# Windowed attention in a fused three-stage kernel: the division moved from the weights to the output, and each engine's order written as a list

## The chip, the cores and the metric

The kernel runs on one core of one Trainium2 chip. The metric is the device time of one execution in microseconds (us), the median of several runs. Engines are named as in the profile: PE (TensorE; PEld is its weight load), DVE (VectorE), ACT (ScalarE), POOL (GpSimd), SP (the queue that issues most DMAs).

## The reference, cut to what matters

```python
# q, k, v: (4, 8, 576, 64), float32
scores = q @ k.T / sqrt(64) - slope[h] * |i - j|      # kept where 0 <= i - j < 128
attn = exp(scores - max)
attn = attn / (sum(attn) + 1e-9)
x = (attn @ v).transpose(0, 2, 1, 3).reshape(4, 576, 512)
x = x + relu(layer_norm(x) @ w_ch1) @ w_ch2           # 512 -> 2048 -> 512
h = relu(x @ w_in)                                    # 512 -> 1024
out = (h * sigmoid(conv3(h))) @ w_out                 # 1024 -> 512
```

The four weight matrices and the convolution's weights come in as 64-bit floats and are turned into float32 on the chip, in integer steps on halves of the words.

## The kernel before, in words

**Attention** comes first. Its unit is a tile: 128 query rows of two heads. Two batches of 576 rows make a block of 9 tiles, and 2 blocks of batches times 4 pairs of heads give 72 tiles. A round of the loop at L873 takes four tiles, as two halves a and b, so there are 18 rounds. For one half:

- `turn_qk`: 8 transposes on PE of q and k into a PSUM buffer (`ps_r`, tag `ptr`), copied out by ACT (`copy_turned`).
- `scores`: 16 products and 8 bias products on PE (64x64 pieces) into `ps_s`; `join` and `minima` on DVE; four `exponentials` on ACT, each with its row sums.
- `shares`: 1/sum on DVE, then the weights `pp` times it, three of the four pieces on DVE (L787), one on POOL (L788).
- `turn_p`: 4 transposes; `copy_p` on ACT; `select_p`: two masks on POOL (L810); `values`: up to 16 products on PE (128x64 pieces) into `po`; `outputs`: copy on ACT into `x`, once a round.

The rounds overlap: round n holds the scores of round n, the turning of P of n-1 and the values of n-2. Every engine takes its instructions in the order in which the loop body calls them; the list of calls is the schedule.

**Beside it** twelve pieces of `w_ch1` and `w_ch2` are loaded (0.5 MB each, SP) and turned into two float32r parts. A piece that is loaded in half-round o has its steps in half-rounds o+3 to o+8 (`FINE_AT`, `FINE_START`): rescale on POOL (L358), three integer steps on DVE (L373, L378, L383), the high part on ACT (L412), the low part on DVE (L415). All starts o are odd, so rescale and the first DVE step stand in one round. The layer norm of the first 384 rows (`LN_ATT`) and two first blocks of the hidden layer (`hidden`) are in the attention loop too.

**After it** (from L958) a planner (`Plan.issue`) writes the rest, with PE as its fixed backbone, into the same queues behind the attention.

`extras` in a round of before calls the weight steps of its first half-round after both joins and minima, and those of the second at the end of the round, ahead of the next round's first join.

Of the kernel before, what the change touches and what calls it, by code (L numbers as in the profile page):

```python
# [210 lines left out]
def tile_kernel(  # L211
# [183 lines left out]
    FINE = (("rescale",), (0,), (1,), (2,), ("high",), ("low",))  # L395

    def weights_step(stages, start=True, only=None):

        now = [ld for ld in reversed(flight) if only in (None, ld["only"])]
        now = [(ld, ld["stages"].pop(0)) for ld in now]  # L400
        for j in range(max((len(do) for _, do in now), default=0)):
            for ld, do in now:
                if j >= len(do):
                    continue
                kind, i, raw = ld["kind"], ld["i"], ld["raw"]
                if do[j] == "rescale":
                    t = ld["t"] = fav(FA_CV0 + cvn[0] % 3 * 512, 512).bitcast(I32)
                    cvn[0] += 1
                    rescale(t, raw, G)
                elif do[j] == "high":  # L410
                    w = wtile(kind, i)
                    S.activation(w[:, 0, :], ld["t"].bitcast(F32), AF.Copy)  # L412
                elif do[j] == "low":
                    w = wtile(kind, i)
                    V.tensor_tensor(  # L415
                        out=w[:, 1, :], in0=ld["t"].bitcast(F32), in1=w[:, 0, :].bitcast(F32),
                        op=ALU.subtract,
                    )
                    flight.remove(ld)
                else:  # L420
                    to_f32(ld["t"], raw, (do[j],), ld["mid"])
        if todo and start:
            kind, i, pool = todo.pop(0)
            raw = scratch["raw"][:, scratch["n"] % 3, :]
            scratch["n"] += 1
            if kind in ("w1", "win"):
                src = (w_ch1 if kind == "w1" else w_in)[:, 2 * i * P : 2 * (i + 1) * P]
                nc.sync.dma_start(
                    raw.rearrange("p (c f) -> p c f", f=2 * P),
                    src.rearrange("(c p) f -> p c f", p=P),  # L430
                )
            else:
                src = (w_ch2 if kind == "w2" else w_out)[i * P : (i + 1) * P, :]
                nc.sync.dma_start(raw, src)
            flight.append({
                "kind": kind, "i": i, "pool": pool, "t": None, "mid": None, "only": only,
                "raw": raw.rearrange("p (n two) -> p n two", two=2), "stages": list(stages),
            })
# [98 lines left out]
    with ExitStack() as actx:  # L537
# [4 lines left out]
        ps_r = actx.enter_context(tc.tile_pool(name="ps_r", bufs=2, space=PSUM))  # L542
        ps_t = actx.enter_context(tc.tile_pool(name="ps_t", bufs=1, space=PSUM))
# [154 lines left out]
        turned = []  # L698
        live = {}

        def turn_qk(n: int):

            qt = qts[n] = apool.tile([P, W], F32, tag="qt", name=f"qt_{n}", bufs=3)
            ptr = ps_r.tile([P, 2, W], F32, tag="ptr", name=f"ptr_{n}")
            for i in range(2):
                for u in range(2):
                    bl, pr, t = seq[n + u]
                    T.transpose(ptr[:, i, u * P : (u + 1) * P], raws["qk"[i], bl, pr, t], ident)  # L708
            kd = kt[:, n % NK : n % NK + 2, :].rearrange("p u j -> p (u j)")
            turned.append((qt, ptr[:, 0], -SCALE))  # L710
            turned.append((kd, ptr[:, 1], 1.0))
# [54 lines left out]
        def exponentials(n: int, parts=range(4)):  # L766
            sc, mn = live["sc", n], live["mn", n]
            if parts[0] == 0:
                live["pp", n] = apool.tile([P, 2, 2, P], F32, tag="pp", name=f"pp_{n}", bufs=4)
                live["sm", n] = apool.tile([P, 2, 4], F32, tag="sm", name=f"sm_{n}", bufs=4)  # L770
            pp, sm = live["pp", n], live["sm", n]
            for i in parts:
# [3 lines left out]
                    accum_out=sm[:, 0, i : i + 1],  # L776
                )

        def shares(n: int):
# [4 lines left out]
            pp = live["pp", n].rearrange("p u h j -> p (u h) j")  # L784
            part = pp[:, 0:3, :]
            r = sm[:, 1, 0:3].rearrange("p (i o) -> p i o", o=1).broadcast_to([P, 3, P])
# [6 lines left out]
        def turn_p(n: int, pool=ps_t, tag="pt"):  # L793
            pp = live.pop(("pp", n))
            ptp = live["ptp", n] = pool.tile([P, 4, P], F32, tag=tag, name=f"ptp_{n}")
# [19 lines left out]
        def values(n: int):  # L815

            pt = live.pop(("pt", n))
            if n % 4 == 0:
                live["po"] = ps_o.tile([P, 4, P], F32, tag="po", name=f"po_{n}")
            po = live["po"][:, n % 4 : n % 4 + 2]  # L820
# [10 lines left out]
        def outputs(n: int):  # L831

            po = live.pop("po")
            cut = next((u for u in range(1, 4) if seq[n + u][1] != seq[n][1]), 4)
            for u0, u1 in ((0, cut), (cut, 4)):
                if u0 < u1:
                    bl, pr, t = seq[n + u0]
                    t += bl * TPB
                    S.activation(xt(t, t + u1 - u0, pr), po[:, u0:u1], AF.Copy)

        fine_at = {}
        for key, o in enumerate(FINE_START):
            for i, at in enumerate(FINE_AT):
                fine_at.setdefault(o + at, []).append((i == 0, key))
# [4 lines left out]
        def copy_turned():  # L849

            for dst, src, scale in turned[:2]:
                S.activation(dst, src, AF.Copy, scale=scale)
            del turned[:2]

        def extras(n: int, m: int):
            for args in fine_at.get(n // 2 + m, ()):
                weights_step(FINE, *args)
            for u in (n + 2 * m, n + 2 * m + 1):
                if u in SMALL_AT:
                    small_inputs(SMALL_AT.index(u))  # L860
                for stage, j in LN_ATT.get(u, ()):
                    layer_norm(0, j, stage, ps_r, "ptr")

        turn_qk(0)
        copy_turned()
        turn_qk(2)  # L870
        load_qk(*seq[TPB][:2], 0)
        load_qk(*seq[TPB][:2], 1)
        for n in range(0, NS, 4):  # L873
            a, b = n, n + 2
            before, last = n > 0, n == NS - 4
            if n // 4 < len(NB):
                keep_busy(NB[n // 4], f"a{n}")
            scores(a)
            if n > 4:
                exponentials(b - 4, range(2, 4))  # L880
            copy_turned()
            scores(b)
            if n >= 8:
                copy_p(b - 8)
                select_p(b - 8)
            if n >= 12:
                outputs(n - 12)
            join(a)
            minima(a)
            if n == 0:  # L890
                turn_qk(a + 4)
                copy_turned()
            join(b)
            minima(b)
            if n > 4:
                shares(b - 4)
            extras(n, 0)
            if n >= 8:
                values(a - 8)
                values(b - 8)  # L900
            exponentials(a)
            exponentials(b, range(2 if 0 < n and not last else 4))
# [1027 lines left out]
```

## Time and profile before

| | |
|---|---|
| median of 3 runs | 733.05 us (731.72 to 734.97) |
| profiled execution, its own time | 734.73 us |
| its span, first to last instruction | 733.0 us |
| busy share PE / PEld / DVE / ACT / POOL | 96 / 90 / 71 / 55 / 31 % |
| attention and its drain, up to the planner's first product | 148.3 us |

Busy shares are averages over stages that differ; an instruction on PE counts as busy from its start to its modelled end, so a busy PE can still have gaps between its weight loads.

### The profile page before, as it was taken

What the parts mean: (1) busy time and instruction counts of PE and PEld (TensorE: products, weight loads), DVE (VectorE), ACT (ScalarE), POOL (GpSimd) and SP (SyncE); (2) the same over time, 40 slices, a digit from 0 to 9 for tenths busy, and PEclk for the clock granted to TensorE, in tenths of its full rate; (3) what the DMA queues carried; (4) which work ended last, traced back from release to release, by engine and by line L of the source; (5) the groups of instructions that cost most, each with busy time, mean ns of one, the idle gap of its engine ahead of it and who ended that gap; (6) DMA issues with size and microseconds to landing.
All of it is one profiled execution on the core that took longest, in us unless ns stands there. A gap on an engine that the chain in (4) does not pass through costs nothing.

```text
span 733.0 us, 14382 instructions
## 1 busy us (share of the span) xinstructions
PE 706.0 (96%) x5200; PEld 657.5 (90%) x5200; DVE 520.0 (71%) x1018; ACT 402.3 (55%) x1050; POOL 230.5 (31%) x372
## 2 busy tenths in 40 slices
PE   6998888899999999999999999999999999999998
PEld 5776766699999999999999999999999899998887
DVE  6789898667888636556778655558469998786730
ACT  4887877655524323334346333344477787776741
POOL 1667688768722102221310223242421000000000
PEclk9999998999999999999999999999999999999999
DMA  6877866247529726977860699996932000000011
GB/s 145 179 186 175 201 155 190 69 156 233 179 98 306 255 77 198 299 232 238 239 207 12 179 289 280 303 279 195 265 94 80 16 30 16 29 23 22 30 54 47
DMA packets 122306, 114.69 MB, mean 156 GB/s; under 512 B 63552, under 2 KB 87292, under 8 KB 122236
## 3 DMA queue, kind: packets, MB, share of 16 engines
q1 hardware_dynamic: 101020, 76.81, 35.1%
q0 software_dynamic: 20160, 36.71, 18.1%
q8 instruction: 41, 0.67, 0.4%
q10 hardware_dynamic: 1056, 0.26, 0.2%
q14 instruction: 29, 0.24, 0.1%
HBM read 80.70 MB, written 33.05 MB: 155 GB/s over the span
## 4 chain that ended last, share of the span: by engine, by line
PE 79%; DVE 8%; POOL 4%; ACT 4%; DMA 2%; issue 2%; POOLq 0%; ACTq 0%; DVEq 0%
PE bank L1049 73%; DMA wind<-r 2%; POOL pt L810 2%; DVE ps L760 2%; ACT pp L774 1%; PE po L826 1%; DVE mn L764 1%; PE ptp L798 1%; POOL pp L788 1%; DVE pp L787 1%; PE bank L1105 1%; PE ps L734 1%; PE ptr L708 1%; ACT fa L1010 1%; DVE fa L378 1%
## 5 line engine op out<-in xcount | busy, mean ns | idle before, releaser
L1049 PE MATMUL bank<-hhr,r 128*128 128x384 f32 x1152 | 213.8, 337 | 0.5 <-DVE fa L1017 0.5
L1049 PE MATMUL bank<-r,r 128*128 128x288 f32 (+1 forms) x1248 | 204.2, 314 | 1.3 <-ACT fa L1010 1.2
L1049 PEld LDWEIGHTS bank<-hhr,r 128*128 128x128 f32 x1152 | 199.1, 188 | 2.6 <-DVE fa L1017 1.5
L1049 PEld LDWEIGHTS bank<-r,r 128*128 128x128 f32 x1248 | 193.9, 188 | 4.5 <-ACT fa L1010 2.6
L1343 POOL DMA_DIRECT2D r<-w1d x96 | 51.6, 538 | 175.1 <-PE bank L1049 158.1
L1010 ACT ACTIVATE fa<-bank 128x288 f32<-128x288 f32 (+1 forms) x112 | 49.7, 443 | 72.5 <-PE bank L1049 71.1
L1049 PE MATMUL bank<-r 128*128 128x512 f32 (+2 forms) x360 | 81.8, 372 | 0.2 <-ACT r L1793 0.2
L1049 PEld LDWEIGHTS bank<-r 128*128 128x128 f32 x360 | 63.6, 188 | 9.9 <-ACT r L1793 0.6
L1010 ACT ACTIVATE r<-fa 128x256 fp32r<-128x256 f32 (+2 forms) x94 | 47.8, 521 | 38.6 <-DMA wind<-r 12.4
L1017 DVE TENSOR_TENSOR fa<-bank,fa 128x288 f32<-128x288 f32 (+1 forms) x88 | 43.5, 500 | 25.2 <-ACT fa L1010 13.6
L1010 ACT ACTIVATE hhr<-bank 128x384 fp32r<-128x384 f32 x46 | 22.5, 490 | 68.7 <-PE bank L1049 68.5
L774 ACT ACTIVATE pp<-ps,mn 128x128 f32<-128x128 f32 x144 | 51.2, 376 | 14.8 <-DVE mn L764 12.7
L1025 DVE SCALAR_TENSOR_TENSOR fa<-fa,cw 128x576 f32<-128x576 f32 x64 | 51.2, 813 | 1.5 <-ACT fa L1010 0.7
L1017 DVE TENSOR_TENSOR r<-fa,r 128x256 fp32r<-128x256 f32 (+1 forms) x74 | 37.6, 520 | 19.3 <-ACT r L1010 13.3
L826 PE MATMUL po<-pt,rawv 128*64 128x128 f32 x544 | 38.9, 283 | 11.0 <-POOL pt L810 8.0
L1025 DVE SCALAR_TENSOR_TENSOR hhr<-bank,hhr 128x384 fp32r<-128x384 f32 x46 | 25.5, 553 | 33.8 <-ACT hhr L1010 33.8
L810 POOL TENSOR_SCALAR_AFFINE_SELECT pt<-pc 128x512 f32<-128x512 f32 x72 | 47.8, 693 | 1.8 <-ACT pc L803 1.5
L826 PEld LDWEIGHTS po<-pt,rawv 128*64 128x64 f32 x544 | 29.5, 138 | 19.9 <-POOL pt L810 17.2
L1049 PE MATMUL bank<-r,hhr 128*128 128x512 f32 (+1 forms) x192 | 44.6, 381 | 0.0
L788 POOL TENSOR_SCALAR pp<-pp,sm 128x128 f32<-128x128 f32 x36 | 34.0, 946 | 32.5 <-DVE sm L783 31.2
L1010 ACT ACTIVATE fa<-fa 128x576 f32<-128x576 f32 (+1 forms) x64 | 39.1, 620 | 2.5 <-DVE fa L1017 1.4
L1049 PEld LDWEIGHTS bank<-r,hhr 128*128 128x128 f32 x192 | 34.1, 188 | 6.7
(149 smaller groups left out, 1105.3 us busy)
## 6 DMA issues: line engine op xcount, KB each, us to landing
r<-w1d POOLq DMA_DIRECT2D x96, 256.0 KB, 4.8
fa<-in_moe_w_ch SPq DMA_DIRECT2D x24, 512.0 KB, 5.6
w1d<-r SPq DMA_DIRECT2D x40, 256.0 KB, 3.1
wind<-r SPq DMA_DIRECT2D x28, 256.0 KB, 5.0
r<-wind POOLq DMA_DIRECT2D x28, 256.0 KB, 4.9
out<-h SPq DMA_DIRECT2D x17, 256.0 KB, 2.0
rawq<-in_q SPq DMA_DIRECT2D x32, 128.0 KB, 3.4
rawv<-in_v SPq DMA_DIRECT2D x32, 128.0 KB, 3.1
```

The source lines that it names most:

```text
L378: V.scalar_tensor_tensor(out=mid, in0=raw[..., 1], scalar=-0x80000000, in1=mid, op0=ALU.bitwise_and, op1=ALU.bitwise_or,)
L708: T.transpose(ptr[:, i, u * P : (u + 1) * P], raws["qk"[i], bl, pr, t], ident)
L760: V.copy_predicated(out=sc, mask=own4, data=ps[:, :, :, P:W])
L774: S.activation(pp[:, u, h, :], sc[:, h, u], AF.Exp, bias=mn[:, h, u : u + 1], scale=-1.0, accum_out=sm[:, 0, i : i + 1],)
L788: G.tensor_scalar(out=pp[:, 3, :], in0=pp[:, 3, :], scalar1=sm[:, 1, 3:4], scalar2=1.0, op0=ALU.mult, op1=ALU.mult,)
L810: G.affine_select(out=parts[:, i], in_=pc, compare_op=ALU.is_ge, fill=0.0, base=base, pattern=[[0, 4], [sign, P]], channel_multiplier=-sign,)
L826: T.matmul(po[h * D : (h + 1) * D, u, :], rvs[bl, pr][:, t - 1 + i, h, :], pt[:, i, 2 * u + h, :], start=i == i0, stop=i == 1,)
L1010: lambda: S.activation(now(out), now(src), func, **kw),
L1017: "V", tt_ns(cols(out)), lambda: V.tensor_tensor(out=out, in0=a, in1=b, op=op),
L1025: lambda: V.scalar_tensor_tensor(out=now(out), in0=now(a), scalar=sc, in1=now(b), op0=op0, op1=op1),
L1049: T.matmul(out, lhs, now(rhs), start=start and n == 0, stop=stop and n == len(items) - 1, skip_group_check=True,)
L1343: plan.add("G", 560, lambda: nc.gpsimd.dma_start(dst, src), [src], [dst], nbytes=262144)
```

## The change

The weights `pp` go unnormalised through `turn_p`, `select_p` and `values`. `ratios` (DVE, once a round, 8 sums) makes the reciprocals; `spread` (POOL) widens them to 128x512; `spread_r` (PE) turns that with four transposes into a `ptr` buffer; `outputs` copies `po` to `x` as before, and `divide` (DVE) multiplies `x` by the turned reciprocals. `turn_p` uses the `ptr` ring, which has three buffers in place of 2 + 1. The high part of a weight piece is made by POOL, not by ACT. The loop over rounds is gone: five lists give each engine's order, a digit after a name says how many rounds behind the list's round it is, and `w0`, `w1` stand for the weight steps of the two half-rounds.

```diff
-    ps_r bufs=2, ps_t bufs=1
+    ps_r bufs=3
...
+    FINE_ON = "GVVVGV"
...
-                    S.activation(w[:, 0, :], ld["t"].bitcast(F32), AF.Copy)
+            G.tensor_copy(w[:, 0, :], ld["t"].bitcast(F32))
...
-        def shares(n: int):
+        def ratios(n: int):
             sm = live["sm", n]
             V.tensor_scalar(out=sm[:, 1], in0=sm[:, 0], scalar1=1e-9, scalar2=None, op0=ALU.add)
             V.reciprocal(out=sm[:, 1], in_=sm[:, 1])
-            V.tensor_tensor(out=part, in0=part, in1=r, op=ALU.mult)
-            G.tensor_scalar(
-                out=pp[:, 3, :], in0=pp[:, 3, :], scalar1=sm[:, 1, 3:4], scalar2=1.0,
-                op0=ALU.mult, op1=ALU.mult,
-            )
+        def spread(n: int):
+            rx = live["rx", n] = apool.tile([P, 4, 2, D], F32, tag="rx", name=f"rx_{n}")
+            G.tensor_copy(
+                out=rx, in_=live.pop(("sm", n))[:, 1].rearrange("p (h u o) -> p u h o", h=2, o=1).broadcast_to([P, 4, 2, D])
+            )
+        def spread_r(n: int):
+            rx = live.pop(("rx", n))
+            bc = live["bc", n] = ps_r.tile([P, 4, P], F32, tag="ptr", name=f"bc_{n}")
+            for u in range(4):
+                T.transpose(bc[:, u, :], rx[:, u].rearrange("p h d -> p (h d)"), ident)
...
+        def divide(n: int):
+            bc = live.pop(("bc", n))
+            for u0, u1, at in parts_of_x(n):
+                V.tensor_tensor(out=at, in0=at, in1=bc[:, u0:u1], op=ALU.mult)
...
+        ORDER = {
+            "T": "bc3 sa0 qa0 qb0 vb2 h0 pb1 pa1 sb0 va2 h1",
+            "V": "ja0 ma0 rat1 w0 w1 jb0 mb0 x2",
+            "S": "ea0.1 pcb2 w0 ea1.1 o3 pca2 eb0.1 eb1.1 cqa0 cqb0 w1",
+            "G": "ta2 w0 tb1 ex1 w1",
+            "L": "l0 w0 l1 w1",
+        }
...
+        def small_work(it):      # layer norm, yielded behind "x" of round it
...
-            scores(a)
...
-            extras(n, 1)
+        while any(streams.values()):
+            eng = min((e for e in streams if streams[e] and ready(e)), key=lambda e: streams[e][0][0])
+            _, nm, _, takes, go = streams[eng].pop(0)
+            go()
```

In the lists bc is `spread_r`, s `scores`, q `turn_qk`, v `values`, h `hidden`, p `turn_p`, j `join`, m `minima`, rat `ratios`, x `divide`, e0 and e1 the two pairs of exponentials, pc `copy_p`, o `outputs`, cq `copy_turned`, t `select_p`, ex `spread`, l the loads of q, k and v.

## Rows read from the trace of the kernel before

**Rows 1.** Windows: four stretches; busy us (xinstructions) of PE, PEld, DVE, ACT, POOL, PEclk

```profile
8.55:84.67 76.12, 66.70 (x1045) 51.87 (x1037) 63.94 (x140) 62.39 (x259) 46.90 (x67) 1.00 0.78 181
84.67:132.39 47.72, 40.43 (x581) 31.71 (x581) 43.79 (x87) 37.27 (x148) 39.05 (x51) 0.93 0.62 158
132.39:148.32 15.93, 12.96 (x133) 10.84 (x133) 8.18 (x19) 8.61 (x28) 12.10 (x19) 1.00 0.25 81
148.32:733.00 584.68, 579.05 (x3378) 556.69 (x3377) 399.42 (x754) 291.55 (x610) 130.61 (x218) 1.00 0.51 155
```

**Rows 2.** Timeline of DVE, parts of two rounds: start us, us, instruction

```profile
42.39 0.69 DVE L760 COPY_PREDICATED ps<-own,ps 128x512 f32<-128x512 int32 x1
43.12 0.69 DVE L764 TENSOR_REDUCE mn<-ps 128x4 f32<-128x512 f32 x1
43.72 0.16 DVE L782 TENSOR_SCALAR sm<-sm 128x4 f32<-128x4 f32 x1
...
44.13 0.56 DVE L787 TENSOR_TENSOR pp<-pp,sm 128x384 f32<-128x384 f32 x1
44.60 0.69 DVE L378 SCALAR_TENSOR_TENSOR fa<-fa 128x512 int32<-128x512 int32 x1
45.21 0.26 DVE L782 TENSOR_SCALAR sm<-sm 128x4 f32<-128x4 f32 x1
...
83.85 0.68 DVE L474 BATCH_NORM_STATS2 st<-px 128x6 f32<-128x512 f32 x1
...
84.67 0.67 DVE L760 COPY_PREDICATED ps<-own,ps 128x512 f32<-128x512 int32 x1
```

**Rows 3.** Windows: two single rounds, first join to first join

```profile
47.49:55.15 7.66, 7.35 (x125) 5.72 (x125) 6.11 (x16) 7.04 (x27) 4.35 (x8) 1.00 0.80 197
...
114.90:124.97 10.07, 8.03 (x76) 6.61 (x80) 7.73 (x15) 6.34 (x26) 10.07 (x13) 0.66 0.92 270
```

**Rows 4.** Timeline of SP: the second and the seventh weight load

```profile
27.39 0.50 SPq L434 DMA_DIRECT2D fa<-in_moe_w_ch  x1
...
77.78 0.44 SPq L428 DMA_DIRECT2D fa<-in_moe_w_ch  x1
```

**Rows 5.** Timeline of POOL: rescales of those loads, and four masks

```profile
32.38 0.65 POOL L358 TENSOR_SCALAR fa<-fa 128x512 f32<-128x512 f32 x1 [1.57 <-DMA fa<-in_moe_w_ch]
...
82.57 0.73 POOL L358 TENSOR_SCALAR fa<-fa 128x512 f32<-128x512 f32 x1 [2.83 <-DMA fa<-in_moe_w_ch]
...
142.22 2.40 POOL L810 TENSOR_SCALAR_AFFINE_SELECT pt<-pc 128x512 f32<-128x512 f32 x4 [0.38 <-PE po L826]
```

**Rows 6.** Timeline of PEld: in brackets the idle time ahead and its releaser

```profile
20.41 0.53 PEld L734 LDWEIGHTS ps<-kt,qt 64*64 64x64 f32 x16 [0.30 <-ACT kt L852]
...
21.44 1.51 PEld L826 LDWEIGHTS po<-pt,rawv 128*64 128x64 f32 x28 [0.20 <-issue]
23.12 0.42 PEld L798 LDWEIGHTS ptp<-ident,pp 128*128 128x128 f32 x4 [0.17 <-issue]
23.51 0.25 PEld L708 LDWEIGHTS ptr<-ident,rawq 128*128 128x128 f32 x2
...
27.52 1.76 PEld L826 LDWEIGHTS po<-pt,rawv 128*64 128x64 f32 x32 [0.20 <-issue]
```

**Rows 7.** Windows of one us at the clock's fall: PE busy, granted clock

```profile
117.00:118.00 1.00, 0.00 (x0) 0.77 1.14 257
...
124.00:125.00 1.00, 1.00 (x28) 0.81 0.56 189
```

**Rows 8.** Timeline of ACT: exponentials and a copy of P

```profile
87.27 0.36 ACT L774 ACTIVATE pp<-ps,mn 128x128 f32<-128x128 f32 x1
...
87.61 0.37 ACT L774 ACTIVATE pp<-ps,mn 128x128 f32<-128x128 f32 x1
...
88.30 0.61 ACT L803 ACTIVATE pc<-ptp 128x512 f32<-128x512 f32 x1
```

**Rows 9.** Timeline of PE in the drain: the first hidden block

```profile
136.48 2.33 PE L524 MATMUL ph<-xna,r 128*128 128x384 f32 x12
```

More of the change, by code (lines that the diff above doesn't have):

```diff
@@ L395, in tile_kernel @@
     FINE = (("rescale",), (0,), (1,), (2,), ("high",), ("low",))
[L397 to L411, printed above, removed]
-                    S.activation(w[:, 0, :], ld["t"].bitcast(F32), AF.Copy)
[L413 to L417, printed above, removed]
-                    )
[L419 to L438, printed above, removed]
@@ new lines, in weights_stage @@
+    def weights_stage(key: int, j: int):
+        ld, stage = flight[key], FINE[j][0]
+        kind, i, raw = ld["kind"], ld["i"], ld["raw"]
+        if stage == "rescale":
+            t = ld["t"] = fav(FA_CV0 + cvn[0] % 3 * 512, 512).bitcast(I32)
+            cvn[0] += 1
+            rescale(t, raw, G)
+        elif stage == "high":
+            w = wtile(kind, i)
+            G.tensor_copy(w[:, 0, :], ld["t"].bitcast(F32))
+        elif stage == "low":
+            w = wtile(kind, i)
+            V.tensor_tensor(
+                out=w[:, 1, :], in0=ld["t"].bitcast(F32), in1=w[:, 0, :].bitcast(F32),
+                op=ALU.subtract,
+            )
+        else:
+            to_f32(ld["t"], raw, (stage,), ld["mid"])
@@ L697, in tile_kernel @@
         half = NS // 2
-        turned = []
+        turned = {}
         live = {}
@@ L868, in tile_kernel @@
         turn_qk(0)
[L869 removed]
+        copy_turned(0)
         turn_qk(2)
+        copy_turned(2)
+        emitted |= {("cqa", -1), ("cqb", -1)}
         load_qk(*seq[TPB][:2], 0)
         load_qk(*seq[TPB][:2], 1)
[L873 to L877, printed above, removed]
[L878 to L930 removed]
@@ L953, in tile_kernel, with ready @@
-        extras(NS + 4, 0)
-        outputs(NS - 4)
-        extras(NS + 4, 1)
+        streams = {eng: list(stream(eng)) for eng in ORDER}
+        first = {("sa", 0): 0, ("sb", 0): 1}
+        streams["T"].sort(key=lambda e: (first.get(e[1], 2)))
+        keep_busy(NB[0], "a0")
+        def ready(eng):
+            _, nm, need, takes, _ = streams[eng][0]
+            past = lambda d: d in emitted or isinstance(d[1], int) and d[1] < 0
+            if nm[0] in ("turn", "gather", "small") and not free("ptr", 3):
+                return False
+            return all(past(d) for d in need) and all(free(r, n) for r, n, _ in takes)
@@ L958, in tile_kernel @@
+        while any(streams.values()):
+            eng = min((e for e in streams if streams[e] and ready(e)), key=lambda e: streams[e][0][0])
+            _, nm, _, takes, go = streams[eng].pop(0)
+            go()
+            emitted.add(nm)
+            for ring, _, by in takes:
+                rings.setdefault(ring, []).append(by)
+            if nm[0] in ("turn", "gather") or nm == ("small", 3):
+                rings.setdefault("ptr", []).append(nm)
     del pools["y"]
```

220 lines of the change are left out of this document (144 added, 76 removed).

## Prediction

> **What bounds the kernel now.** I read the windows of four stretches first [rows 1]. From 148.3 us on the PE is busy 579.05 of 584.68 us on work that the change does not touch; so whatever the attention gains or loses arrives at the end unchanged, and the question is only when PE can start that work. Ahead of it lie three stretches: eleven rounds from the first join at 8.55 to 84.67 (76.12 us, 6.9 a round), six rounds to 132.39 (47.72 us, 7.95 a round), and the drain (15.93 us from the last round's first join).
>
> Next I read the timelines of DVE, POOL and SP. In the six rounds DVE is busy 43.79 of 47.72 us [rows 1]: it is the bound there. In the first stretch it is busy 63.94 of 76.12, and rounds alternate: those in which a weight piece has its rescale are long (7.66 us, [rows 3]) because POOL stands still for the load. The second load is issued at 27.39 and its rescale starts at 32.38 after a wait on DMA; the seventh at 77.78 and 82.57, after 2.83 us of waiting [rows 4, 5]. From issue to rescale that is 4.99 and 4.79 us: the rescale starts as the load lands. SP issues the q, k and v loads in the same queue without a longer pause up to there, so this stretch is paced by SP's order and not by an engine. The trace of PE then gives the cost of its parts, and the windows around 117 us show the one place where its clock fell [rows 6, 7].
>
> **The change part by part.**
>
> *DVE.* One 128x512 join takes 0.73 us start to start, a minimum 0.60, the addition and reciprocal 0.41, the multiplication of three weights pieces 0.47, an integer step 0.61 [rows 2]. A round with four weight steps was 2 x (0.73 + 0.60) + 2 x (0.41 + 0.47) + 4 x 0.61 = 6.9. After: 2.66 + 0.41 + 2.44 + one product of 128x512. That product is not in the trace; below stands the 0.60 of a one-pass 128x512 reduction, above the 0.69 busy of an integer step; I take 0.65. Sum 6.15, so 0.75 us less a round. Where the six rounds ran at 7.95, the rest was layer norm work (0.82 us from a statistics instruction to the join behind it) and one fall of the clock.
>
> *POOL and ACT.* POOL loses two pieces of weights a round and gains a widening and, per weight piece, a copy. Neither stands in the trace; the nearest one-input 128x512 rows are the masks (0.60 each) and the rescale (0.65 to 0.73) [rows 5]. With 0.65 each a full round is 4 x 0.60 + 3 x 0.65 = 4.35 us; even at double price for the new two (5.65) POOL is not the bound. ACT loses the high part: no gain, since PE and DVE stand ahead of it (62.39 busy in 76.12 [rows 1], much of it overlapped records).
>
> *PE.* Four more transposes cost 0.42 [rows 6]. The order costs more. Each time PE goes from 64x64 scores to 128x64 values to 128x128 transposes there is an idle gap, 0.17 to 0.20 us, with nothing to wait for but issue [rows 6]. Before, a round has three such changes: scores a and b, values a and b, all transposes. The new list has seven: bc, sa, q, vb, p, sb, va are each of another kind than their neighbour. Five of the seven are of kinds that the rows show with their gap; from scores straight to transposes (sa to q) and from transposes straight to values (q to vb) the old order never goes, so there the price lies between nothing and 0.20 us. I take 0.17 to 0.20 for these too, as for every change that the trace has. Work per round from the rows: scores 2 x 0.83 (20.41 to 21.44 less the gap), values 1.76, transposes 4 x 0.42 + 0.42 = 2.10 (q and k 0.84, P 0.84, bc 0.42): 5.5 us. With three gaps PE's floor was 5.6 with the old work; with seven it is 6.7 to 6.9, with five 6.4. I take 6.8, above DVE's 6.15. The Trainium skill's TensorEngine Tiling (Key Properties) says that switching the tiling mode, not just the tile, drains the TensorE: a rule against an order that mixes the kinds. By it all seven changes cost a gap (6.8 us a round), by the kinds that the rows show alone five (6.4), which over six rounds would be 2.4 us less. So PE replaces DVE as the bound of an undisturbed round. Lower bound, if the gaps hide behind the earlier wait: DVE's 6.15.
>
> *The first stretch.* SP's order of loads is the same, and the loads before the seventh leave SP back to back, so I keep 77.78 for its issue and 82.57 for its rescale. What changes is what stands behind it. Before, the first integer step came at the round's end and the next round's first join followed (84.67). After, `w1` stands ahead of `jb mb x2`: rescale to 83.2, integer step 0.61, low part of an earlier piece 0.61, join 0.73, minimum 0.60, product 0.65, and two statistics of the layer norm with 0.82 each, which are yielded behind the product: the next first join at 88.0, **3.4 us later**. What is queued behind the late rescale on POOL (`tb`, then values on PE) and on DVE (`jb`, then exponentials, then P on PE) waits with it. The gain of the undisturbed rounds in this stretch only makes the next wait for a load longer. Lower bound, if the loads land early enough: two short first rounds to about 17.5, nine of 6.8 and 1.6 of statistics, 80.3, which is 4.4 us earlier than before.
>
> *The six rounds.* 6 x 6.8 = 40.8, and 1.2 us for a turn and a gather of the layer norm with their gaps and their place in the three-buffer ring: 42.0 against 47.72, **5.7 us less**. Bounds: 6 x 6.15 + 1.2 = 38.1, and 47.7 if the clock falls again and contention eats the rest.
>
> *The drain.* From the last round's first join: vb 1.05 with its gap, two P turns 1.0, sb 1.0, so the second join starts at 3.1 and its minimum ends at 4.4. Meanwhile va ends at 4.1, the output copy at 4.7 (0.61 [rows 8]), the product at 5.35, two normalised parts on DVE (0.6 each) at 6.5. Only then can `h0` run, which stands ahead of `pb1` in PE's list: 12 products, 2.2 us of the 2.33 [rows 9], to 8.7. Its two results are put into ACT's queue ahead of the second half's exponentials: one 0.5, a copy of P 0.5, four exponentials at 0.34 each [rows 8], 11.1. Then P turned 12.0, copied 12.1, masked 13.3, the widening 13.95, two more masks 15.15, values 16.2, `h1` 18.4, the last bc 19.0. Before it was 15.93: **3.1 us more**. Bounds: 15 (the hidden blocks overlap as before) and 21.
>
> **Sum.** +3.4 - 5.7 + 3.1 = +0.8 us. On the profiled execution's own time, 734.73 (span 733.0 and 1.7 around it), that is 735.5; that execution lies 1.7 above the median of the runs, 733.05, so for a median I give 733.9, rounded **734**. What a measurement here can tell from no change is about 0.5%, 3.7 us.
>
> **The rivals.**
>
> *Faster: the loads do not pace it.* If the seven late loads land in time, the first stretch is worth -4.4 in place of +3.4, and the total is 734 - 7.8 = **726**. For it: in the new list q and k are turned right behind the scores, earlier in the round, which frees the buffers of SP's next loads earlier. Against: up to 78 us SP has no pause that such a buffer would shorten. A second way to the same side: the gaps of the PE hide, and the six rounds run at 6.15 (-3.9) and the drain's six gaps at nothing (-1.0): **729**. Together 0.34.
>
> *Slower: the clock falls in the waits.* In the trace PE did nothing from 117 to 118 us after two short waits for masks, and the granted clock went from 1.00 to 0.50 (2.4 to 1.2 GHz) and came back in the 124th microsecond [rows 7]; the round around it took 10.07 us at 0.66 [rows 3]. At half rate for some 6.4 us of work the fall costs 6.4 / 2, less the first idle part: 2.9 us. After the change each late load stops POOL ahead of `tb` and DVE ahead of `jb`, so PE has only one half of values (0.88) to do in some 4.5 us. The skill's TensorE: Matmul & The Clock Gate (HAM oscillation) tells of this pattern: waits for DMA between bursts of products bring the lower clock back each time. Five of the seven loads were late before; part of each fall hides in the wait for the next load. Against: the waits of the same rounds before brought no fall. From two falls that are not hidden it decides: 734 + 2 x 2.9 = **740**. Chance 0.28.
>
> *No change, as summed:* 0.38. That the division does not leave the bound is no rival of its own: the pieces of `shares` that go are certain, only what then bounds is not.
>
> **Numbers.** Faster by over 0.5% (below 729.4) 0.34, within 0.5% 0.38, slower 0.28. The range has to take in both other cases: below 726 lies some spread of the first rival, so 722; above 740 a third fall, so 742. The likeliest case's own range, from the bounds of the drain and of PE's gaps, is 730 to 738.
>
> **What would show it.** Right: `ptr`, `ps` and `po` weight loads with 0.17 to 0.20 us of idle time ahead at seven places of a round; rounds of some 6.8 us behind 88 us with DVE no longer the releaser; rescales that wait for DMA up to the seventh, and joins behind them; `h0` waiting for the parts, and the second half's exponentials behind it; the planner's first product near 149 us. Wrong: first joins at or ahead of the old times by the twelfth round (SP was not the pace), rounds near 6.2 (gaps hidden), a drain of 16 us, or granted clocks of 0.50 in the first 85 us. A planner stretch that is not 584.7 us long would break the first sentence.

## The result, and the profile after

The changed kernel takes **743.4 us** (median of 4 runs, 741.5 to 746.9), the kernel before 732.75 beside it: a ratio of 1.0147 [1.010, 1.0193]. The forecast was 734 us, with a range of 722 to 742. The profiled execution is the longest of the four (746.93 us, span 745.1). Its four stretches are those of [rows 1], cut in the same way (busy us of PE, PEld, DVE, ACT, POOL, then the granted clock, DMA share and GB/s):

```profile
8.03:86.95 78.92, 72.97 (x1058) 56.91 (x1050) 59.32 (x109) 60.09 (x255) 43.56 (x65) 0.96 0.79 182
86.95:134.75 47.80, 43.02 (x620) 32.92 (x620) 40.97 (x72) 34.48 (x141) 33.34 (x49) 1.00 0.62 167
134.75:154.81 20.06, 16.84 (x154) 13.16 (x153) 7.55 (x18) 8.74 (x29) 9.61 (x16) 0.91 0.05 17
154.81:745.10 590.29, 580.99 (x3377) 558.19 (x3377) 398.62 (x755) 290.83 (x609) 130.26 (x218) 1.00 0.50 154
```

DVE is relieved, if by less than forecast: in the six rounds it is busy 40.97 us instead of 43.79 [rows 1], 2.8 us less where 0.75 a round would be 4.5, and PE takes its place as the busiest. But the six rounds are as long as before, although the fall of the clock that the kernel before has in them [rows 7] is not there. Single rounds, first join to first join, show why: the thirteenth to the sixteenth.

```profile
94.96:104.43 9.47, 6.27 (x93) 4.46 (x89) 6.90 (x13) 4.15 (x17) 8.88 (x16) 1.00 0.42 109
104.43:110.79 6.36, 6.22 (x101) 4.96 (x102) 5.89 (x13) 5.62 (x25) 3.47 (x6) 1.00 0.57 132
110.79:117.53 6.74, 6.74 (x101) 5.37 (x102) 6.37 (x11) 5.60 (x25) 4.26 (x7) 1.00 0.79 202
117.53:126.93 9.40, 8.60 (x128) 6.85 (x128) 8.12 (x13) 5.55 (x25) 9.08 (x11) 1.00 0.44 115
```

The fourteenth takes 6.36 us with PE busy 6.22, the fifteenth 6.74 with PE busy in all of it: these are the forecast's rounds. In the thirteenth and the sixteenth POOL is the engine that is busy nearly throughout, 8.88 of 9.47 and 9.08 of 9.40. Its timeline in the thirteenth:

```profile
95.14 0.20 POOL L480 TENSOR_SCALAR w<-mv 128x3 f32<-128x3 f32 x1 [3.34 <-DVE mv L472]
...
97.66 0.20 POOL L486 TENSOR_TENSOR mv<-w 128x3 f32<-128x3 f32 x1
97.81 1.23 POOL L812 TENSOR_SCALAR_AFFINE_SELECT pt<-pc 128x512 f32<-128x512 f32 x2
99.01 0.66 POOL L358 TENSOR_SCALAR fa<-fa 128x512 f32<-128x512 f32 x1
```

and DVE's beside it:

```profile
96.59 0.64 DVE L378 SCALAR_TENSOR_TENSOR fa<-fa 128x512 int32<-128x512 int32 x1
99.70 0.81 DVE L373 TENSOR_SCALAR fa<-fa 128x512 int32<-128x512 int32 x1 [2.46 <-POOL fa L358]
100.43 1.12 DVE L383 SCALAR_TENSOR_TENSOR fa<-fa 128x512 int32<-128x512 int32 x1
101.47 1.12 DVE L430 TENSOR_TENSOR r<-fa,r 128x512 fp32r<-128x512 f32 x1
102.51 0.68 DVE L755 COPY_PREDICATED ps<-own,ps 128x512 f32<-128x512 int32 x1
```

POOL waits 3.34 us for the layer norm's statistics, then works on its square root from 95.14 to 97.86, and only then come mask and rescale. DVE waits 2.46 us for this rescale, and the second join, ready at about 97.6 when PE ended its scores, starts at 102.51. No load is late here.

The late seventh load of the first stretch went as forecast: rescale at 80.90 after a wait for DMA (compare [rows 5]), `w1` ahead of the second join, and the next first join at 86.95 (forecast 88.0, before 84.67 [rows 2]).

```profile
80.90 0.67 POOL L358 TENSOR_SCALAR fa<-fa 128x512 f32<-128x512 f32 x1 [2.72 <-DMA fa<-in_moe_w_ch]
...
82.06 1.88 POOL L812 TENSOR_SCALAR_AFFINE_SELECT pt<-pc 128x512 f32<-128x512 f32 x2
```

```profile
81.60 0.80 DVE L373 TENSOR_SCALAR fa<-fa 128x512 int32<-128x512 int32 x1 [2.46 <-POOL fa L358]
82.33 1.11 DVE L430 TENSOR_TENSOR r<-fa,r 128x512 fp32r<-128x512 f32 x1
83.36 0.68 DVE L755 COPY_PREDICATED ps<-own,ps 128x512 f32<-128x512 int32 x1
...
86.95 0.67 DVE L755 COPY_PREDICATED ps<-own,ps 128x512 f32<-128x512 int32 x1
```

The first two rounds are where this profile's first stretch got longer: from the first join at 8.03 to the third round's at 22.73 it is 14.70 us, before 11.86; the other nine rounds take 64.2 us, before 64.3. In the new list `qa0` stands right behind `sa0`; PE stands still for the exponentials and then for a load of q, and the clock, which stays at 1.00 there in the kernel before, is at 1.2 GHz from 15.0 to 21.9 us:

```profile
12.23 0.88 PE L729 MATMUL ps<-kt,qt 64*64 64x192 f32 x16 [2.26 <-ACT pp L770]
15.40 0.45 PE L704 MATMUL ptr<-ident,rawq 128*128 128x128 f32 x1 [1.81 <-DMA rawq<-in_q]
```

```profile
14.00:16.00 2.00, 0.60 (x2) 0.29 (x2) 1.10 (x4) 0.00 (x0) 0.00 (x0) 0.76 0.75 169
18.00:20.00 2.00, 2.00 (x15) 1.57 (x17) 0.00 (x0) 2.00 (x10) 0.20 (x1) 0.50 0.52 119
```

All profiles of the new lists have a fall of some 7 us in this place, and their first two rounds take 13.2 to 14.8 us. With the division in the order of before (runs 4, 8 and 11) the fall lasts 3.5 us and the two rounds take 12.4 to 12.6.

### The profile page after: what moved, and what is told of

The parts are those of the page before. It is cut to its first block, busy times and chain, and to the rows that moved or that the text cites. A ratio compares the mean times of both kernels' runs of the same rounds, so it can differ in the third digit from the quotient of the medians.

```text
span 745.1 us, 14474 instructions
## 1 busy us (share of the span) xinstructions
PE 720.4 (97%) x5272; PEld 667.6 (90%) x5272; DVE 510.9 (69%) x970; ACT 396.6 (53%) x1038; POOL 218.7 (29%) x366
## 4 chain that ended last, share of the span: by engine, by line
PE 73%; DMA 10%; DVE 6%; ACT 5%; SPq 2%; POOL 2%; issue 2%; ACTq 0%; DVEq 0%; POOLq 0%
PE bank L1113 66%; DMA wind<-r 5%; DMA fa<-in_moe_w_ch 3%; PE po L828 2%; PE ptp L800 1%; ACT pp L770 1%; SPq L559 1%; POOL pt L812 1%; PE ps L729 1%; DVE fa L1081 1%; PE bank L1169 1%; ACT fa L1074 1%; DMA fa<-w1f 1%; DVE fa L383 1%; DVE r L430 1%
## 5 line engine op out<-in xcount | busy, mean ns | idle before, releaser
L1113 PE MATMUL bank<-r 128*128 128x512 f32 (+2 forms) x360 | 81.8, 372 | 0.2 <-ACT r L1857 0.2
L812 POOL TENSOR_SCALAR_AFFINE_SELECT pt<-pc 128x512 f32<-128x512 f32 x72 | 51.2, 734 | 47.8 <-ACT pc L805 47.7
L770 ACT ACTIVATE pp<-ps,mn 128x128 f32<-128x128 f32 x144 | 52.8, 395 | 13.7 <-DVE mn L759 10.1
L1113 PE MATMUL bank<-xn,r 128*128 128x384 f32 x192 | 35.9, 336 | 0.0
```

The source lines that it names most:

```text
L770: S.activation(pp[:, u, h, :], sc[:, h, u], AF.Exp, bias=mn[:, h, u : u + 1], scale=-1.0, accum_out=sm[:, 0, 4 * h + n % 4 + u : 4 * h + n ...
L812: G.affine_select(out=parts[:, i], in_=pc, compare_op=ALU.is_ge, fill=0.0, base=base, pattern=[[0, 4], [sign, P]], channel_multiplier=-sign,)
L1113: T.matmul(out, lhs, now(rhs), start=start and n == 0, stop=stop and n == len(items) - 1, skip_group_check=True,)
```

## The experiments

All lengths are read in the same way: from the first join to the twelfth round's, to the eighteenth's, to the planner's first product, to the end. Times are medians; ratios are to the kernel before, run on the same chip, with medians of 732.8 us beside runs 1 to 4 and 9 to 12 and 734.1 beside runs 5 to 8. The lengths of the stretches come from one profile each.

| kernel | first | six rounds | drain | planner | us | ratio |
|---|---|---|---|---|---|---|
| before | 76.1 | 47.7 | 15.9 | 584.7 | 732.8 | 1 |
| changed | 78.9 | 47.8 | 20.1 | 590.3 | 743.4 | 1.0147 [1.010, 1.0193] |
| 1 weights last | 81.8 | 49.1 | 20.0 | 585.6 | 746.8 | 1.0186 [1.0155, 1.0218] |
| 2 layer norm on POOL later | 80.3 | 44.1 | 20.0 | 584.0 | 739.4 | 1.0083 [1.0052, 1.0113] |
| 3 hidden block later | 82.4 | 47.1 | 18.8 | 586.1 | 742.6 | 1.0122 [1.0086, 1.0159] |
| 4 division alone | 75.7 | 46.6 | 21.9 | 585.6 | 740.3 | 1.0093 [1.0061, 1.0126] |
| 5 steps later | 78.2 | 48.6 | 19.3 | 584.1 | 740.4 | 1.0081 [1.0053, 1.0109] |
| 6 values merged | 84.0 | 54.4 | 19.6 | 588.1 | 754.2 | 1.0273 [1.0235, 1.0312] |
| 7 busy drain | 79.7 | 47.0 | 18.6 | 584.7 | 741.6 | 1.0094 [1.0064, 1.0125] |
| 8 division, hidden last | 76.7 | 53.3 | 20.6 | 589.5 | 748.1 | 1.0187 [1.0147, 1.0228] |
| 9 = 5 + rows' load earlier | 78.2 | 44.4 | 19.5 | 586.3 | 738.2 | 1.0061 [1.0038, 1.0084] |
| 10 = 9 + 2 + 3 + fillers | 76.6 | 43.4 | 18.0 | 584.3 | 733.4 | 1.0011 [0.999, 1.0031] |
| 11 division, hidden between | 77.9 | 47.2 | 22.1 | 586.5 | 743.6 | 1.0122 [1.0078, 1.0167] |
| 12 = 5 without the division | 75.0 | 47.5 | 18.6 | 585.3 | 735.7 | 1.0039 [1.0019, 1.0059] |

Up to the twelfth round, the changed kernel and runs 2, 3 and 7 run the same instructions in the same order on each engine: their 78.9, 80.3, 82.4 and 79.7 show the spread of one program, mean 80.4.

**1. Weight steps behind the second join**

```diff
-            "V": "ja0 ma0 rat1 w0 w1 jb0 mb0 x2",
+            "V": "ja0 ma0 rat1 jb0 mb0 x2 w0 w1",
```

> The changed kernel with one edit: VectorE's list ends in jb mb x2 w0 w1, so both weight steps of a round stand behind the second join and the division instead of ahead of them. Theory A (the weight step ahead of jb is what cost the rounds with a late rescale): no second join waits for a rescale any more, so round 12 (9.47 us) comes back towards the 6.4 to 6.7 us of the undisturbed rounds 13 and 14, round 15 (9.40) by half, and the waits of 2.46 us ahead of the first integer step are paid behind the joins; the attention ends at about 148 to 151 us instead of 154.8 and the ratio to the changed kernel is 0.991 to 0.996, about 737 to 740. Rival B (TensorE's kind-changes and the division's extra turns cost it): the attention ends within 1 us of 154.8, since TensorE's work is the same. Rival C (the loads pace the first stretch whatever the list): the twelfth round's first join stays within 1 us of 86.95 and only the six rounds behind it get shorter.

A miss for A: no faster, the median 3 us above the changed kernel's with intervals that overlap; the attention's end at 159.44 us and the twelfth round's first join at 90.33 lie outside the bands of B and C too. From the sixth round on the second joins come 1.6 to 2.4 us behind the first, yet most rounds take 6.7 to 8.3 us. DVE now waits ahead of the product instead, 12.7 us in all (8.2 of them ahead of the drain) for ACT's copies of the outputs where it was 0.3:

```profile
110.17 0.93 DVE L852 TENSOR_TENSOR x<-x,bc 128x128 f32<-128x128 f32 x2 [0.59 <-ACT x L846]
111.02 0.68 DVE L378 SCALAR_TENSOR_TENSOR fa<-fa 128x512 int32<-128x512 int32 x1
```

ACT copies the outputs behind the first half's exponentials; in the changed order the weight steps fill that time on DVE, here they come behind the product and the next round's first join behind them. So this other place is no better, and what the steps wait for, the late loads, stays as it was.

**2. POOL's layer-norm work behind mask, rescale and cast**

```diff
+                    if (stage in ("root", "minus")) != pool:
+                        continue
...
+                    if eng == "V" and name == "w" and late == "1" and it:
+                        for nm, need, go in small_work(it - 1, True):
+                            yield key, nm, need, [], go
```

> The changed kernel with one edit: GpSimd's share of the layer norm (the square root and the subtractions of the mean) is queued behind the round's mask, rescale and cast instead of ahead of them. Theory A (GpSimd's layer-norm work, waiting for its own inputs, holds the mask and the rescale, and these hold the second join): rounds 12 and 15, 9.47 and 9.40 us, come back to 7 to 8 us, the six rounds from 47.8 to 43 to 45 us, the time from 743 to 739 to 741. Rival B (the extra TensorE and VectorE work of the layer norm itself fills these rounds): the six rounds stay within 1 us of 47.8. The first stretch, 8.0 to 86.95 us, stays as it is by both.

As A expected: the six rounds fall by 3.7 us, the thirteenth from 9.47 to 5.65, the time by 4. The sixteenth (9.18) is not mended.

**3. First hidden block behind the last turns of weights**

```diff
-            "T": "bc3 sa0 qa0 qb0 vb2 h0 pb1 pa1 sb0 va2 h1",
+            "T": "bc3 sa0 qa0 qb0 vb2 pb1 pa1 h0 sb0 va2 h1",
```

> The changed kernel with one edit: TensorE's list has the first hidden block behind the turns of the last weights, bc3 sa0 qa0 qb0 vb2 pb1 pa1 h0 sb0 va2 h1. Theory A (the hidden block stands ahead of the last turns and delays the last outputs): the drain from the last round's first join to the planner's first product goes from 20.06 to 17.5 to 18.5 us and the time falls by about 2. Rival D (the drain is held by the late exponentials and by the clock, which falls when TensorE idles in them): the drain stays within 1 us of 20.06, because without the hidden block TensorE idles longer and the second hidden block runs at half the clock.

Between the two: the drain is 1.2 us shorter, and the clock falls all the same (the hidden block takes 3.39 us where it took 2.36).

**4. The division alone, in the order of before**

```diff
-    FINE_ON = "GVVVGV"
+    FINE_ON = "GVVVSV"
...
+            "T": "h0 sa0 sb0 h1 va2 vb2 bc3 pa1 qa0 qb0 pb1",
+            "V": "ja0 ma0 jb0 mb0 rat1 w0 x3 w1",
+            "S": "eb1.1 cqb1 pcb2 o3 w0 ea0.0 ea1.0 eb0.0 pca1 cqa0 w1",
+            "G": "tb2 w0 ta1 ex1 w1",
```

> The kernel before with the division of the change alone: the sums are taken over four units, GpSimd widens the reciprocals, TensorE turns them, VectorE multiplies the outputs; each engine's order is that of the kernel before, and ScalarE makes the weights' high part as before. Theory A (the division is not what cost the time, the new orders are): the first stretch is as before (next first join at 84 to 86 us), the six rounds go from 47.7 to 43 to 46 us, since VectorE does 1.5 us less in each and TensorE needs about 6.1 us, the drain lengthens by up to 2 us, and the time is 728 to 734. Rival B (the division costs it: its turns on TensorE and the wait of the outputs for the spread reciprocals): the time is 738 to 745, about that of the changed kernel.

The first stretch is as A expected and the six rounds 0.6 above its band, the two together 1.6 us shorter than before; the time is B's, because the drain is 6.0 us longer, not 2. There PE does nothing for 2.4 us and then runs at 1.2 GHz (windows of 2 us, the clock is third from the end):

```profile
139.00:141.00 2.00, 0.00 (x0) 0.00 (x0) 0.93 (x3) 2.00 (x8) 0.45 (x1) 0.74 0.00 0
141.00:143.00 2.00, 1.87 (x18) 1.90 (x20) 0.00 (x0) 0.03 (x1) 0.78 (x2) 0.50 0.00 0
143.00:145.00 2.00, 2.00 (x19) 1.67 (x16) 0.00 (x0) 0.00 (x0) 0.00 (x0) 0.50 0.03 8
```

**5. Weight steps half a round later behind their load**

```diff
-    FINE_AT = (0, 3, 4, 5, 6, 7, 8)
+    FINE_AT = (0, 4, 5, 6, 7, 8, 9)
```

> The changed kernel with one edit: every step that makes a weight block (rescale, three integer steps, high and low part) comes half a round later behind its load, the lists staying as they are. Late loads (theory A's first half: the rescale waits 1.2 to 3.3 us for its load in each variant so far, and 6 to 7.5 us of the round stand behind it): the rescale's waits for its load go to nothing or below 0.5 us, the first stretch falls from the 78.9 to 82.4 us of the three profiles of this program to 74 to 77, and the time from 743 to 737 to 740. Rival B (TensorE's own work, busy 73 to 75.5 us of that stretch, sets it): the waits go but the stretch stays at 78 or more and the time within 2 us of 743.

The waits go (six rescales of the first stretch start without one, the seventh waits 0.79 us) and the ratio falls to 1.0081, yet the first stretch keeps 78.2: the waits go, as both expected, the stretch stays, as B expected, and the time lies between their bands. An undisturbed round is 6.73 us with PE busy in all of it:

```profile
106.27:113.00 6.73, 6.73 (x101) 5.37 (x100) 6.41 (x13) 5.59 (x24) 5.18 (x9) 1.00 0.74 180
```

One round got worse, the sixteenth, 12.89 us. POOL waits for the layer norm's rows, with the masks behind it:

```profile
119.31 1.95 POOL L504 TENSOR_TENSOR xm<-x,fa 128x384 f32<-128x384 f32 x2 [5.04 <-DMA fa<-rows]
121.22 2.40 POOL L812 TENSOR_SCALAR_AFFINE_SELECT pt<-pc 128x512 f32<-128x512 f32 x4
```

**6. Values merged, five changes of kind instead of seven**

```diff
-            "T": "bc3 sa0 qa0 qb0 vb2 h0 pb1 pa1 sb0 va2 h1",
+            "T": "vb2 bc3 sa0 qa0 qb0 h0 pb1 pa1 sb0 va2 h1",
```

> The changed kernel with one edit: in TensorE's list vb2 goes to the front, vb2 bc3 sa0 qa0 qb0 h0 pb1 pa1 sb0 va2 h1, so that a round's first products of the values follow the last ones of the round before and its turns stand in one run: five changes of kind in a round in place of seven. Rival B (each change of kind costs 0.17 to 0.20 us and TensorE sets the rounds): the undisturbed rounds fall from 6.4 to 6.7 us to 6.0 to 6.3, eighteen rounds give 5 to 7 us back, the time goes to 736 to 738. Theory A (waits set the rounds, TensorE's gaps lie in them): the rounds change by less than 0.2 us each and the time stays within 2 us of 743; if the values now wait for the masks behind a late rescale, it gets longer by 1 to 3.

Slower by some 10 us, more than either theory gave. An undisturbed round is 7.35 us, in which PE waits 0.81 for masks and its weight loads 1.05:

```profile
122.56 0.88 PE L828 MATMUL po<-pt,rawv 128*64 128x128 f32 x12 [0.81 <-POOL pt L812]
122.56 0.63 PEld L828 LDWEIGHTS po<-pt,rawv 128*64 128x64 f32 x12 [1.05 <-POOL pt L812]
```

Without the loads' wait it would be 6.3. It holds 28 products of values where the changed kernel's fifteenth round holds 32, and four more take 0.2 (0.63 us of loads for 12, 0.85 for 16), so like for like I estimate 6.5, that is 0.2 less than 6.74: two changes of kind at 0.1 each, less than the 0.17 to 0.20 of [rows 6]. The mixed order costs gaps and hides the latency of the masks; the second is worth more.

**7. Fillers ahead of the last turn of weights**

```diff
+            if n == NS - 2:
+                for i in range(14):
+                    T.transpose(ptp[:, i % 4, :], ident, ident)
```

> The changed kernel with one edit: ahead of the last turn of weights TensorE turns the identity fourteen times into the tile that the turn then overwrites (about 0.13 us each), so that it does not idle while ScalarE makes the last exponentials. Rival D (the clock falls to 1.2 GHz for 3.7 us in the drain because TensorE idles there, and this costs about 2.2 us): the granted clock stays at 1.00 in that stretch, the drain goes from 20.06 to 17.5 to 18.5 us, the time down by 1.5 to 2.5. Theory A (the drain is the order of the hidden block and the exponentials): the drain stays within 0.7 us of 20.06, the clock up or not, because the fillers only fill or lengthen the wait.

In the changed kernel the clock is at 1.2 GHz in the drain (first two rows, changed kernel); with the fillers it stays up (third row, this run):

```profile
145.00:147.00 2.00, 2.00 (x15) 1.67 (x16) 0.15 (x1) 0.60 (x1) 1.00 (x2) 0.50 0.00 0
147.00:149.00 2.00, 1.94 (x19) 1.40 (x17) 0.22 (x1) 0.96 (x2) 0.78 (x2) 0.71 0.00 0
```

```profile
146.00:148.00 2.00, 2.00 (x25) 1.60 (x24) 0.19 (x1) 0.96 (x2) 1.10 (x2) 1.00 0.00 0
```

The drain is 1.45 us shorter, just short of D's band: that is what keeping the clock up is worth here, the fillers' own time included.

**8. As 4, hidden blocks behind the turns**

```diff
-            "T": "h0 sa0 sb0 h1 va2 vb2 bc3 pa1 qa0 qb0 pb1",
+            "T": "sa0 sb0 h1 va2 vb2 bc3 pa1 qa0 qb0 pb1 h0",
```

> The kernel before with the division of the change alone, as in the run above of that name, and the hidden blocks moved behind the turns of weights in TensorE's list (sa0 sb0 h1 va2 vb2 bc3 pa1 qa0 qb0 pb1 h0). Theory A: with the division alone the two stretches ahead of the drain were 1.6 us shorter than before (75.67 and 46.60 against 76.12 and 47.72) and the whole loss lay in the drain (21.9 against 15.9), where TensorE stood first at the hidden block, waiting for the layer norm, and fell to 1.2 GHz for 6 us; moved, the drain is 16 to 18.5 us and the time 733 to 737. Rival B (the division itself costs it): the time stays at 738 to 741 with the drain above 20 us, because the last outputs wait for sums, spread, turn and division whatever stands beside them.

Both miss in the time, and of their numbers only B's drain above 20 us holds; the sixteenth round takes 14.64 us. The edit of PE's list also moved a load on SP, since all queues are written from one merged sequence: the layer norm's rows go out at 114.68 us, in run 4 at 100.74. POOL waits 4.81 us for them, PE 6.68 for the masks behind. The drain is 1.3 us shorter.

**9. As 5, the load of the layer norm's rows one unit earlier**

```diff
-        50: (("gather", 0),), 52: (("spread", 0),),
+        50: (("gather", 0),), 51: (("spread", 0),),
```

> The changed kernel with the steps a half-round later, as in the run above of that name, and one edit more: the load that spreads the layer norm's rows is put at unit 51 instead of 52, so that it is queued right behind the store of these rows and not behind a further round's loads of values. Theory A (in the changed kernel this load goes out at 113 to 115 us instead of 103.1, because its step now comes once in four units; GpSimd's subtraction waits for it, 5.04 us in the run with later steps, and the masks stand behind it): it goes out by 106, the subtraction waits less than 0.5 us, the sixteenth round falls from 12.89 to 7 to 8.5 us and the time from 740.4 to 735 to 737. Rival E (the round is long because of the layer norm's work itself and the clock): the round stays above 10 us and the time within 1.5 us of 740.4.

As A expected in its place, the time a little above its band: the ratio goes from 1.0081 to 1.0061, with intervals that overlap; the planner's stretch of this profile is 2.2 us longer than run 5's. The load on SP before, in the changed kernel and here:

```profile
103.07 0.38 SPq L502 DMA_DIRECT2D fa<-rows  x1
```

```profile
113.11 1.48 SPq L499 DMA_DIRECT2D fa<-rows  x1
```

```profile
102.16 0.38 SPq L499 DMA_DIRECT2D fa<-rows  x1
```

POOL's subtraction starts at 113.87 without a wait, the sixteenth round is 7.96 us instead of 12.89, the six rounds are 4.2 us shorter.

**10. All that helped, together: the edits of 9, 2 and 3, and eight fillers as in 7**

```diff
-            "T": "bc3 sa0 qa0 qb0 vb2 h0 pb1 pa1 sb0 va2 h1",
+            "T": "bc3 sa0 qa0 qb0 vb2 pb1 pa1 h0 sb0 va2 h1",
...
+                for i in range(8):
+                    T.transpose(ptp[:, i % 4, :], ident, ident)
```

> The changed kernel with all that helped so far: steps a half-round later, the rows' load at unit 51, GpSimd's layer-norm work behind the mask, rescale and cast, the hidden block behind the last turns, and eight turns of the identity ahead of the last turn of weights. Theory A (the loss is waits that the new lists make, and they add): first stretch 77 to 79 us, six rounds 41.5 to 43.5, drain 16.5 to 18, the time 729 to 734, level with the kernel before or just below. Rival B (TensorE's longer round sets the floor: 6.74 us in the run with later steps, where nothing else is waited for, against 5.83 to 6.04 in the kernel before): the first stretch stays above 78 us, the six rounds above 43, the time at 734 to 737.

733.4 us, level with the kernel before and in A's band, like the six rounds and the drain; the first stretch is 0.4 below its band. Of B's numbers only the six rounds above 43 hold. Its attention ends at 147.07 us instead of 154.81:

```profile
9.18:85.74 76.56, 73.55 (x1073) 57.85 (x1067) 54.58 (x107) 60.37 (x257) 38.84 (x64) 0.96 0.79 180
85.74:129.11 43.37, 41.44 (x611) 32.16 (x606) 40.28 (x71) 33.83 (x140) 33.59 (x50) 1.00 0.68 172
129.11:147.07 17.96, 17.20 (x161) 13.63 (x162) 8.14 (x18) 7.76 (x27) 9.28 (x15) 0.90 0.21 70
```

PE is busy 114.99 of the 119.93 us of the first two stretches, 96%: what is left there is mostly its own work, some 7 us of it at 1.2 GHz, because the clock falls from 14.1 to 21.0 us here too.

**11. As 4, the first hidden block between the products of values**

```diff
-            "T": "h0 sa0 sb0 h1 va2 vb2 bc3 pa1 qa0 qb0 pb1",
+            "T": "sa0 sb0 h1 va2 h0 vb2 bc3 pa1 qa0 qb0 pb1",
```

> The kernel before with the division alone, as in the run above of that name, and one edit: the first hidden block stands between the two products of values, sa0 sb0 h1 va2 h0 vb2 bc3 pa1 qa0 qb0 pb1, so that its results come behind the last exponentials and the outputs in ScalarE's queue. Theory A (in that drain the hidden block's results stood ahead of the last exponentials and the outputs, and TensorE idled 2.4 us and fell to 1.2 GHz for 6 us): the clock stays up, the drain goes from 21.9 to 16.5 to 18.5 us, the time from 740 to 734 to 737. Rival B (the division's own chain, sums, spread, turn, product, makes the drain long): it stays above 20 us and the time above 738.

A miss: the drain stays at 22.1, and drain and time are B's. PE now waits 3.5 us ahead of the values, until ACT's copy of the outputs ends at 141.11 us and their one buffer is free (POOL's copy that the row names had ended at 140.53), and the hidden block behind takes 4.21 us at 1.2 GHz, the second 2.33:

```profile
141.20 1.97 PE L828 MATMUL po<-pt,rawv 128*64 128x128 f32 x16 [3.50 <-POOL rx L784]
143.10 4.21 PE L521 MATMUL ph<-xna,r 128*128 128x384 f32 x12
```

That copy starts at 140.40, behind two normalised parts, the last exponentials and a copy of P. So in this order it is ACT's queue that empties PE here, whatever the place of the hidden block. How much of the drain is the division's own chain, as B has it, stays open: no run changes ACT's list.

**12. As 5, without the turns and the product: the outputs are left undivided**

```diff
-            for u in range(4):
-                T.transpose(bc[:, u, :], rx[:, u].rearrange("p h d -> p (h d)"), ident)
...
-                V.tensor_tensor(out=at, in0=at, in1=bc[:, u0:u1], op=ALU.mult)
```

> The changed kernel with the steps a half-round later, without the turns of the spread reciprocals on TensorE and without the multiplication on VectorE: the outputs are left undivided. Rival B (TensorE's work sets the rounds once the late loads no longer hold anything): each round loses the turn's 0.66 us and one change of kind, the undisturbed rounds fall from 6.74 to 5.9 to 6.1 us and the first stretch from 78.2 to 70 to 72. Theory F (the loads on the sync engine's queue set the first stretch, as in the kernel before with its 76.1 us): the undisturbed rounds fall, but the first stretch stays at 75 to 77, since the seventh weight load goes out at 76 to 78 us in each variant so far.

F's numbers, at the edge of its band: undisturbed rounds fall from 6.74 to 6.15 us, just short of B's band, the first stretch only by 3.2 to 75.0, and rescales wait for DMA again (2.89 and 2.34 us). So PE and the loads bind that stretch at nearly the same length. (The six rounds hold a sixteenth of 13.16 us, with the late load of run 5.)

## Why the prediction was wrong

**The step that failed is the six rounds**: forecast 42.0 us, measured 47.8 (47.3 in the mean of the three profiles, with runs 3 and 7, that run the same instructions there). The undisturbed round was right (6.8 forecast, 6.36 and 6.74 measured); the term "1.2 us for a turn and a gather of the layer norm" was mis-sized, it is 47.8 less 6 x 6.6, some 8 us. It counted the layer norm's work on PE and DVE and not where the new lists put its POOL and SP parts. Behind the product of a four-unit round, the square root stands ahead of mask and rescale, and the rescale holds the second join (run 2 gives 3.7 us back); the load of its rows goes out 10 us later, and POOL's subtraction, and the masks behind it, wait for it (run 9 gives 4.2 us back where that wait was 5.04; in the changed kernel it is 1.46). In runs 3 and 7, the same instructions in this stretch, it is 0.43 us and nothing, and the sixteenth round 8.32 and 8.07. These savings do not add: with the weight steps later (run 5) the thirteenth round is 7.03 us already. With both mended, run 10's six rounds are still 43.4 us, so of the 8 us some 3.8 stay where 1.2 was forecast, and no run takes those apart. The prediction followed the moved weight steps through every queue, and these two stages through none.

**The first stretch** came out near its forecast in size, +3.4 forecast, +2.8 measured in the profile and +4.2 in the mean of four, but in part by luck. What stands behind the late seventh load is right: from its rescale to the next first join it is 6.05 us, 5.4 forecast, 2.1 before. The first two rounds, for which the sum has nothing, add 2.8 us in the profile and 2.2 in the mean, with the clock at 1.2 GHz for 6.9 us; the prediction itself named granted clocks of 0.50 in the first 85 us as a sign of being wrong. No run changes this place alone. Without late loads the stretch is 78.2, 78.2 and 76.6 us in runs 5, 9 and 10, which run the same instructions up to there, mean 77.7: the loads make 2.7 of the 4.2. What is left of the 4.2 lies in the first two rounds, since the other nine take 63.9 us in the mean of these runs and 64.3 before. PE's work binds those nine all the same: run 12, without the turns and the product, has 61.7 there.

**The drain** was right in mechanism: forecast +3.1, measured +4.2. The hidden block's place is worth 1.2 us (run 3); the unforeseen part is the fall of the clock, 1.45 us (run 7).

**PE's gaps**: the forecast round of 6.8 holds. In the undisturbed round all seven changes of kind show 0.17 or 0.20 us of idle time ahead of the weight loads, the two kinds that the old order never has too; from scores to transposes and from transposes to values it is

```profile
110.68 0.20 PEld L704 LDWEIGHTS ptr<-ident,rawq 128*128 128x128 f32 x2 [0.20 <-issue]
111.70 0.85 PEld L828 LDWEIGHTS po<-pt,rawv 128*64 128x64 f32 x16 [0.17 <-POOL pt L812]
```

But taking two of the seven out saved some 0.1 us each, and the order that saves them is slower (run 6). The rule of the Trainium skill's TensorEngine Tiling (Key Properties), that a switch of the mode drains the engine, agrees with a gap at all seven; as a reason against the mixed order it did not decide.

**DVE's relief** is real and worth little: run 4 shows 1.6 us over seventeen rounds, and not all of that need be DVE's, since the clock's fall in the six rounds of before [rows 7] is not in run 4's. PE and the loads bind right behind DVE.

**The planner's stretch** shifts unchanged in most profiles (584.0 to 586.5), but is 588.1 to 590.3 in three, the changed kernel's among them. In these PE is idle longer in the windows in which DMA is busiest; in the changed kernel's profile its longest wait there is 2.78 us at 499.76, and the clock is at 1.2 GHz for 3.5 us behind it. No run tests why. It accounts for the profiled execution lying above the others, and the median's 10.6 us are not fully closed: the stretches give 4.2 - 0.4 + 4.2 = 8.0, with the means of the profiles of one program, the rest is this stretch and the start.

**The rival "the clock falls in the waits"** came nearest in time, 740, but not by its mechanism: the clock does fall, in the second round, where PE waits for exponentials and a load of q, and in the drain, where it waits for exponentials. In this profile it falls behind no late weight load: it stays at 1.00 from 22 us to the end of the six rounds. (In runs 3 and 7 it falls once more, for 3.5 us behind the thirteenth round.)

## What to carry to other kernels

When orders are rewritten as lists, each stage that rides along with a moved step must be followed on every queue that it issues to: here a square root of 2.7 us and one small load cost more than the division saved. A list for one engine can move the issue order of another, so compare all queues. And before an engine is relieved, see what stands right behind it: here TensorE and the loads did, and even with four of the waits mended the change ends level. The first rounds deserve the same look as the steady ones: here they cost some 2 us that the sum did not have.

## What the runs showed of the hardware

DVE's steps on weights take longer when POOL works at the same time. With the steps at other places beside POOL's work, the same instructions take (mean ns behind the busy us), changed kernel first, then run 5:

```profile
L430 DVE TENSOR_TENSOR r<-fa,r 128x512 fp32r<-128x512 f32 x12 | 11.6, 968 | 0.0
L383 DVE SCALAR_TENSOR_TENSOR fa<-fa 128x512 int32<-128x512 int32 x12 | 10.0, 830 | 0.1
L373 DVE TENSOR_SCALAR fa<-fa 128x512 int32<-128x512 int32 x12 | 7.7, 643 | 9.3 <-POOL fa L358 9.3
```

```profile
L430 DVE TENSOR_TENSOR r<-fa,r 128x512 fp32r<-128x512 f32 x12 | 8.2, 679 | 0.0
L383 DVE SCALAR_TENSOR_TENSOR fa<-fa 128x512 int32<-128x512 int32 x12 | 8.1, 673 | 0.0
L373 DVE TENSOR_SCALAR fa<-fa 128x512 int32<-128x512 int32 x12 | 4.5, 375 | 0.0
```

That is 0.7 us for a weight block of these three steps, and POOL's pair of masks goes from 1.22 to 1.88 us beside them (at 82.06 above). The Trainium skill's SBUF — State Buffer (SBUF: two separate sides) says that a VectorE instruction with two SBUF inputs, or in a two-port mode, and a GpSimd instruction that reads SBUF take turns on one pair of ports, the later one waiting for the other's whole instruction. The lengthening of both agrees with turns; whether it is the whole instruction these rows do not show, nor in which mode the step of L373, which has one input, runs. The forecast priced each step by rows without such a neighbour.
